# Early q and k without zeros in two halves of rows, early v in one transfer a batch

## The chip, the cores and the metric

The kernel runs on one core of a Trainium2 chip. The metric is the device time of one execution in microseconds; the median of the runs is compared. The engines are TensorE (PE, with its weight loads as PEld), VectorE (DVE), ScalarE (ACT), GpSimd (POOL) and SyncE (SP), which issues nearly all transfers.

## The reference

Causal attention with a bias from cumulated sums, then two gated expert layers, the first behind an RMS norm:

```python
# q, k, v: (4, 8, 576, 64), s: (4, 8, 576)
scores = q @ k.T / 8
bias = -(cum[:, :, :, None] - cum[:, :, None, :])      # cum = cumsum(max(s, 0))
scores = where(causal, -1e9, scores + minimum(bias, 0))
x = softmax(scores) @ v                                # to (2304, 512)
xn = x / sqrt(mean(x * x) + 1e-6) * rms_g
y = (silu(xn @ w_gate) * (xn @ w_val)) @ w_out         # d_ff = 1536
out = (silu(y @ w2_gate) * (y @ w2_val)) @ w2_out
```

## The kernel before, in words

The 2304 tokens are cut so that the first 128 queries of each batch are done first, as "early" attention. They need only the first 128 keys, so a group of four heads fits into one PSUM bank. Such a group is a quad (class `EarlyQuad`); there are eight, two for each of the four batches. With their result the first expert layer starts (`moe1("E", ...)`), while the remaining queries (class `Head`, `Unit`, `PairTile`) are attended batch by batch beside it. The later stages (the second half of the first layer and the second layer, by a scheme of seven products) are not touched.

A quad does the following. `load` brings its q and k. `scores` (line 918) makes, for each head, a matmul of q with k (line 922) and one of the bias (line 925, from the tile `heights`, which holds cumulated sums of s), then on VectorE a reduction that adds the mask and takes the row's least (line 930), and on ScalarE the exponential (line 935). `values` transposes the four results on TensorE (line 947), copies them (lines 951 and 952), multiplies them by v (line 956), and copies the result into x (lines 966 and 967). Two heads share the 128 rows of a tile: an even head has its 64 dimensions on rows 0 to 63, an odd one on rows 64 to 127, and zeros stand in the other half, so that one matmul with the keys of both heads gives only one head's scores. For v it is the same with columns: a head's 64 columns stand beside 64 columns of zeros, and two heads add up in one bank.

Before the change, q and k of a quad (`qe`) come from the host with the zeros: 128 rows of six blocks of 128 columns, 384 KB in one transfer (line 910). v comes in two transfers a batch (line 914, 128 KB each, in pieces of 256 B, even and odd heads), into a tile in which a set-up operation, `pad` (line 530), has put the zeros: two memsets of 128x256.

After four quads, and again after the last four, `normalise` makes the RMS norm for two batches: squares on ScalarE (line 990), sums on TensorE (line 997), small steps on VectorE (lines 1050 to 1081) with a power on GpSimd (line 1084), a transposition (line 1093), a spreading matmul (line 1104), then the scaled x and its two parts xH and xL (lines 1108, 1111, 1113). The expert layer's matmuls are line 1124. For the first five of its twelve slices of 128 hidden columns (HALVES = 5), these 512 tokens are taken in two halves of 256, so that the first half can start before the second normalisation is done.

Weights come as 64-bit numbers, two transfers of 512 KB a slice (line 473), and are converted by ScalarE (477, 484), VectorE (479, 488) or GpSimd (485, 488). Their raw tiles use places that are free early: slice 4's raw places are those of the v of batches 0 and 1, slice 5's those of the v of batches 2 and 3, and slices 6 to 9 have those of the quads' q and k.

The order on every engine is written by a planner (class `Plan`), which runs when the kernel is built. Each call of `op` names an engine (or several, the first free one takes it; a second choice stands 1e6 behind in due time), a cost in ns, what is read and written, and a due time `pri`. The planner plays the program through with these costs and always gives a free engine the ready operation with the least due time. The engines then run their lists strictly in that order. SP is one of them: its transfers are issued in the planner's order, and a transfer that must wait holds those behind it. Due times that matter here: quad i has 2i, its value part 2i - 0.6, its loads 2i - 1000; the load of v of a batch had the load's time of its first quad plus 1; weight slice 0 has -990, slices 1 to 4 -985.9, -985.8, -985.7 and -985.6, later ones -982.6 and up; the expert layer 1e4. Set-up operations come by their due time too: `ident` -1.4e6, the bias's `units_` -1.35e6, `mask` -1.3e6, the pads -1.2e6, `cumulate` (the cumulated sums, VectorE, as soon as s is there) -1e6, two clears of conversion places (cvy, line 495) 2, two clears of xH (line 543) 4.5. The planner takes s as there at once, since the ACT queue's transfer costs it 450 ns. Sixteen fillers (line 1256, identity matmuls with due time 1e9, two instructions each) go where the planner sees TensorE idle after the fourth quad. Eleven warm-up matmuls (line 557) precede the first quad.

Of the kernel before, what the change touches and what calls it, by code (L numbers as in the profile page):

```python
# [23 lines left out]
P = 128  # L24
# [309 lines left out]
def tile_kernel(  # L334
# [174 lines left out]


    early_q = [buf("w", f"{z}{f}", [P, 6, P], F32, "eq") for f in range(8, KF) for z in "HL"]
    early_v = [buf("w", f"{z}{f}", [P, NH, 2, D], F32, "ev") for f in (6, 7) for z in "HL"]
    early = [buf("at", f"pTB{i}", [P, 1536], F32, f"early{i}") for i in range(2)]
    early_p = [Part(b, "p", lambda t: t[:, 1024:1536]) for b in early]
    cum = Part(early[0], "cum", lambda t: t[:NB * NH, :S])
# [6 lines left out]
    def setup():  # L522
# [1 line left out]
            make_identity(nc, ident())  # L524
        op(POOL, 700, make_const, w=[ident], pri=-1.4e6)
        op(POOL, 100, lambda en: en.memset(minus_half(), -0.5), w=[minus_half], pri=-0.8e6)
        for i, v in enumerate(early_v):
            def pad(en, v=v):
                for z in range(2):
                    en.memset(v()[:, z::2, 1 - z], 0.0)  # L530
            op([(POOL, 520), (DVE, 620)], 0, pad, w=[(v, "pad")], pri=-1.2e6 + i)

        def units_(en):
            en.memset(f32(unit()[64:]), 0.0)
# [359 lines left out]
    class EarlyQuad:  # L894
# [12 lines left out]

        def load(self, pri):
            b, ql, vl = self.b, self.ql, self.vl
            op(SP, 4 * P * 768, lambda en: en.dma_start(out=ql(), in_=qe[b, self.j]),  # L910
               w=[ql], pri=pri)
            if self.j == 0:
                for z in range(2):
                    op(SP, 6 * P * 256, lambda en, z=z: en.dma_start(
                        out=vl()[:, z::2, z], in_=ve[b, :, z]), w=[(vl, z)], pri=pri + 1 + 0.1 * z)

        def scores(self, pri):
            pt = ps_ring("sps", 2)
            for h in range(4):
                c = slice(P * h, P * h + P)  # L920
                n = 4 * self.i + h
                op(PE, 0.422 * 4 * P, lambda en, h=h, c=c: en.matmul(
                    pt()[:, c], self.ql()[:, h], self.ql()[:, 4 + h // 2],
                    start=True, stop=False), r=[self.ql], w=[pt], pri=pri)
                op(PE, C_TR, lambda en, c=c, n=n: en.matmul(
                    pt()[:, c], unit()[:, n:n + 1].to_broadcast([P, P]), cumHL(),
                    start=False, stop=True), r=[unit, cumHL, (heights, "clear")], w=[pt], pri=pri)
            for h in range(4):
                c = slice(P * h, P * h + P)
                op(DVE, c_tt(P), lambda en, h=h, c=c: en.tensor_tensor_reduce(  # L930
                    out=self.sc()[:, c], in0=pt()[:, c], in1=mask(), scale=-SCALE, scalar=3.0e38,
                    op0=ALU.add, op1=ALU.min, accum_out=self.col()[:, 0, h:h + 1]),
                   r=[pt, mask], w=[(self.sc, h), (self.col, h)], pri=pri)
                g = 4 * self.j + h
                op(ACT, c_act(P, 2) + 35, lambda en, h=h, c=c, g=g: en.activation(
                    self.sc()[:, c], self.sc()[:, c], ACTF.Exp, scale=-1.0,
                    bias=self.col()[:, 0, h:h + 1],
                    accum_out=self.tot()[:, self.b % 2, g:g + 1]),
                   r=[(self.sc, h), (self.col, h)],
                   w=[(self.sc, h), (self.tot, (self.b, g)), *([f"early {self.i}"] if h == 3 else [])],  # L940
                   pri=pri)

        def values(self, pri):
            pt = ps_ring("tp", 2)
            for h in range(4):
                c = slice(P * h, P * h + P)
                op(PE, C_TR, lambda en, c=c: en.transpose(pt()[:, c], self.sc()[:, c], ident()),
                   r=[(self.sc, h), ident], w=[pt], pri=pri)
            p = self.p
            op([(ACT, c_act(512)), (DVE, c_tt(512))], 0, {  # L950
                ACT: lambda en: en.activation(p(), pt(), ACTF.Copy),
                DVE: lambda en: en.tensor_copy(p(), pt())}, r=[pt], w=[p], pri=pri)
            po = mo_bank()
            for h in range(4):
                c = slice(P * (h // 2), P * (h // 2) + P)
                op(PE, 0.422 * 4 * P, lambda en, h=h, c=c: en.matmul(
                    po()[:, c], self.vl()[:, 4 * self.j + h].rearrange("p z d -> p (z d)"),
                    p()[:, P * h:P * h + P], start=h % 2 == 0, stop=h % 2 == 1),
                   r=[self.vl, p], w=[po], pri=pri)

            x, k, q = self.x.bufs[0], 2 * self.j, P * self.b

            def out():
                return x()[:, k:k + 2, q:q + P], po()[:, :2 * P].rearrange("p (k c) -> p k c", k=2)
            op([(ACT, c_act(256)), (DVE, c_tt(256))], 0, {
                ACT: lambda en: en.activation(*out(), ACTF.Copy),
                DVE: lambda en: en.tensor_copy(*out())},
               r=[po], w=[key for g in range(2) for key in self.x.keys(k + g, (self.b,))], pri=pri)
# [986 lines left out]
```

## Time and profile before

| | |
|---|---|
| time, median of 3 runs | 1030.57 us (1030.27 to 1032.48) |
| time of the profiled execution | 1033.18 us |
| its span | 1030.9 us |
| TensorE busy | 1021.2 us, 99% of the span |
| VectorE, ScalarE, GpSimd busy | 764.9, 631.9, 265.3 us |
| granted TensorE clock | full speed in all 40 slices |
| DMA over the span | 212.07 MB, 206 GB/s |

The profile comes from one execution; what lies between its span and its time is start and end. A busy TensorE is not always useful: fillers and warm-up count as busy. The engine lists are in order, so an instruction that waits holds all behind it on its engine. In the timeline rows below, the columns are the start in us, the duration in us, engine, line, operation, output and inputs, the shape, the number of instructions merged into the row, and in brackets the idle time ahead of it and what ended it. SPq rows are issues of transfers.

### The profile page before, as it was taken

The numbers are of one execution on the slowest core, as the hardware profiler recorded it, in microseconds if no ns is written. First come the engines' busy times: TensorE is split into PE (matmuls) and PEld (weight loads), VectorE is DVE, ScalarE is ACT, GpSimd is POOL, SyncE is SP. The second block draws the span as 40 slices with busy tenths as digits, with TensorE's granted clock in tenths as the row PEclk, the third lists the DMA queues.
The fourth block names the chain that finished last, engine by engine and source line by source line (L and its number), as shares of the span: only waits on it lengthen the run. The fifth ranks groups of instructions, "written<-read, shape, count | busy, mean of one in ns | idle before, by whom it ended". The sixth has DMA issues, their size and how long they took to land.

```text
span 1030.9 us, 17596 instructions
## 1 busy us (share of the span) xinstructions
PE 1021.2 (99%) x5546; PEld 901.6 (87%) x5546; DVE 764.9 (74%) x1748; ACT 631.9 (61%) x1315; POOL 265.3 (26%) x357
## 2 busy tenths in 40 slices
PE   9999999999999999999999999999999999999998
PEld 9998889999999999899888889888888888778888
DVE  7899887677778796568889896566768667866462
ACT  6889876766677465334567765455655445665653
POOL 3678754444344430100000000212211022200000
PEclk9999999999999999999999999999999999999999
DMA  9874534343444773488888643756757766888772
GB/s 330 276 255 136 186 120 121 121 137 105 122 132 146 219 251 139 148 250 297 267 295 274 215 147 101 248 203 211 255 185 248 267 219 232 296 274 254 214 241 94
DMA packets 122717, 212.07 MB, mean 206 GB/s; under 512 B 19008, under 2 KB 46912, under 8 KB 122624
## 3 DMA queue, kind: packets, MB, share of 16 engines
q1 hardware_dynamic: 122288, 210.61, 62.6%
q8 instruction: 44, 0.72, 0.3%
q14 instruction: 49, 0.40, 0.1%
q10 hardware_dynamic: 336, 0.34, 0.1%
HBM read 146.33 MB, written 64.56 MB: 205 GB/s over the span
## 4 chain that ended last, share of the span: by engine, by line
PE 86%; DMA 6%; DVE 5%; issue 1%; ACT 1%; SPq 1%; POOL 0%; DVEq 0%; ACTq 0%; POOLq 0%
PE mo L1124 24%; PE mo L1486 9%; PE mo L1667 9%; PE sps L1667 7%; PE sps L1486 6%; PE tp L1486 6%; PE tp L794 4%; PE sps L712 3%; PE tp L782 3%; PE mo L1743 2%; DMA raw<-in_w_gv 2%; PE mo L1540 2%; PE sps L1124 1%; PE tp L1124 1%; PE sps L837 1%
## 5 line engine op out<-in xcount | busy, mean ns | idle before, releaser
L1124 PE MATMUL mo<-xH,L 128*128 128x448 f32 (+2 forms) x472 | 170.2, 361 | 0.2 <-DVE L L488 0.2
L1124 PE MATMUL mo<-xL,H 128*128 128x448 f32 (+2 forms) x472 | 169.5, 359 | 0.5 <-DVE xL L1113 0.5
L1124 PE MATMUL mo<-xH,H 128*128 128x448 f32 (+2 forms) x472 | 169.4, 360 | 0.0
L749 ACT ACTIVATE sc<-sc,col 128x256 f32<-128x256 f32 (+2 forms) x96 | 60.6, 632 | 59.2 <-DVE col L738 58.7
L1124 PEld LDWEIGHTS mo<-xL,H 128*128 128x128 f32 x472 | 88.9, 188 | 6.0 <-DVE xL L1113 0.7
L1124 PEld LDWEIGHTS mo<-xH,L 128*128 128x128 f32 x472 | 88.9, 188 | 5.9 <-DVE L L488 0.4
L1124 PEld LDWEIGHTS mo<-xH,H 128*128 128x128 f32 x472 | 88.8, 188 | 5.0
L1406 DVE TENSOR_TENSOR hL<-hh,hH 128x512 fp32r<-128x512 f32 (+1 forms) x96 | 64.2, 673 | 38.0 <-ACT hH L1403 37.3
L1403 ACT ACTIVATE hH<-hh 128x512 fp32r<-128x512 f32 (+1 forms) x96 | 57.6, 603 | 52.2 <-DVE hL L1406 20.4
L1486 PE MATMUL mo<-hH,wo 128*128 128x512 f32 x208 | 68.6, 390 | 0.0
L787 DVE TENSOR_TENSOR pTB<-tp,pTB 128x512 fp32r<-128x512 f32 (+1 forms) x96 | 56.3, 597 | 14.3 <-ACT pTB L785 13.6
L1673 ACT ACTIVATE u<-sps 128x512 f32<-128x512 f32 x48 | 28.5, 594 | 53.3 <-PE sps L1667 51.3
L785 ACT ACTIVATE pTB<-tp 128x512 fp32r<-128x512 f32 (+1 forms) x96 | 48.5, 517 | 14.5 <-PE tp L782 13.8
L794 PEld LDWEIGHTS tp<-pTB,vst 128*128 128x128 f32 x320 | 52.9, 189 | 4.2 <-DVE pTB L787 0.8
L794 PE MATMUL tp<-pTB,vst 128*128 128x448 f32 (+3 forms) x320 | 55.3, 314 | 0.1
L782 PE MATMUL tp<-ident,sc 128*128 128x128 f32 x320 | 51.3, 273 | 0.1
L1682 ACT ACTIVATE u<-u 128x512 f32<-128x512 f32 x48 | 29.5, 631 | 32.4 <-DVE u L1677 32.4
L1630 POOL TENSOR_TENSOR tmp<-x,x 128x512 f32<-128x512 f32 x2 | 2.6, 1298 | 171.9 <-DVE x L1502 115.5
L1486 PEld LDWEIGHTS mo<-hH,wo 128*128 128x128 f32 x208 | 39.1, 188 | 8.1
L726 POOL TENSOR_SCALAR_AFFINE_SELECT sc<-cb 128x128 f32<-128x128 f32 x96 | 35.6, 386 | 38.7 <-PE tp L782 37.7
L782 PEld LDWEIGHTS tp<-ident,sc 128*128 128x128 f32 x320 | 39.6, 140 | 6.3 <-PE mo L1124 0.4
L738 DVE CUSTOM_DVE_ANT_0 sc<-sps,cb 128x256 f32<-128x256 f32 (+2 forms) x96 | 35.6, 383 | 11.7 <-PE sps L712 11.6
(318 smaller groups left out, 3017.8 us busy)
## 6 DMA issues: line engine op xcount, KB each, us to landing
raw<-in_w_gv SPq DMA_DIRECT2D x44, 511.8 KB, 5.9
tb<-h_d SPq DMA_DIRECT2D x48, 256.0 KB, 3.4
t<-tb SPq DMA_DIRECT2D x48, 256.0 KB, 3.0
lq<-in_qk SPq DMA_DIRECT2D x32, 288.0 KB, 3.9
cb<-cum_d SPq DMA_DIRECT2D x32, 288.0 KB, 3.7
h<-t SPq DMA_DIRECT2D x32, 256.0 KB, 3.3
h<-h_d SPq DMA_DIRECT2D x24, 256.0 KB, 3.6
row0B<-u SPq DMA_DIRECT2D x24, 256.0 KB, 3.5
```

Source lines behind the costliest of these rows:

```text
L726: op(POOL, 165 + 0.85 * m, lambda en: en.affine_select(out=sc()[:m, o:o + m], in_=cb()[:m, o:o + m], pattern=[[-1, m]], base=0, compare_op ...
L738: op(DVE, c_tt(w), lambda en: en.tensor_tensor_reduce(out=sc()[:m, c:c + w], in0=pt()[:m, c - at:c - at + w], in1=bias()[:m, c + off:c + o ...
L749: op(ACT, c_act(o + m, 2) + 35, lambda en: en.activation(sc()[:m, :o + m], sc()[:m, :o + m], ACTF.Exp, scale=-1.0, bias=col()[:m, 0, t:t + 1],
L782: op(PE, C_TR, lambda en, pt=pt, a=a, kb=kb, t=t: en.transpose(pt()[:, a * P:a * P + P], self.sc[t]()[:, kb * P:kb * P + P], ident()), r=[ ...
L785: op(ACT, c_act(n), lambda en, pt=pt, c=c: en.activation(place(H, c), source(pt, c), ACTF.Copy), r=[pt], w=[(H, c)], pri=pri)
L787: op(DVE, c_tt(n), lambda en, pt=pt, c=c: en.tensor_tensor(out=place(L, c), in0=source(pt, c), in1=f32(place(H, c)), op=ALU.subtract), r=[ ...
L794: op(PE, c_mm(n), lambda en, w=w, z=z, kb=kb, d0=d0, n=n, o=o: en.matmul(po()[:, o:o + n], vst[j]()[:, kb, :], pT[z]()[:, d0:d0 + n], star ...
L1124: op(PE, c_mm(n), lambda en, a=a, x=x, c=c, k=k, i=i: en.matmul(ps()[:, :n], a()[:, c], x(k, lo, n), start=(k == 0 and i == 0), stop=(k == ...
L1403: op(ACT, c_act(n) + 35, lambda en: en.activation(H(), src(), ACTF.Copy), r=[src, *after], w=[H], pri=pri)
L1406: lambda en: en.tensor_tensor(out=L(), in0=src(), in1=f32(H()), op=ALU.subtract),
L1486: op(PE, c_mm(n), lambda en, m=m, w=w, xx=xx, kk=kk, i=i: en.matmul(ps[m]()[:, :n], w(), xx(), start=first and kk == 0 and i == 0, stop=kk ...
L1667: op(PE, c_mm(n), lambda en, w=w, xx=xx, cut=cut, kk=kk, i=i: en.matmul(ps()[:, :n], W[w]()[:, cut], xx(), start=first and kk == 0 and i == 0,
```

## The change

Three things change. The zeros of q and k no longer come from the host: a quad's tile of six blocks is loaded in two transfers of 64 rows and four blocks each (128 KB), and eight `pad` operations (two memsets of 64x256 each) set the zeros on the chip. The matmuls take the same shapes from other blocks. v of a batch comes in one transfer of 384 KB, 3 KB a row, with a block of zeros between the two heads of a pair; no pad is needed for it. Its due time is the first quad's load plus 2.5 instead of plus 1, and the pads have -1.3e6 and -1.3e6 + 1 for the first two quads and 2i - 3.5 for the others.

```diff
--- before.py
+++ after.py
@@ -509,7 +509,7 @@
 
 
     early_q = [buf("w", f"{z}{f}", [P, 6, P], F32, "eq") for f in range(8, KF) for z in "HL"]
-    early_v = [buf("w", f"{z}{f}", [P, NH, 2, D], F32, "ev") for f in (6, 7) for z in "HL"]
+    early_v = [buf("w", f"{z}{f}", [P, NH // 2 * 3 * D], F32, "ev") for f in (6, 7) for z in "HL"]
     early = [buf("at", f"pTB{i}", [P, 1536], F32, f"early{i}") for i in range(2)]
     early_p = [Part(b, "p", lambda t: t[:, 1024:1536]) for b in early]
     cum = Part(early[0], "cum", lambda t: t[:NB * NH, :S])
@@ -524,11 +524,12 @@
             make_identity(nc, ident())
         op(POOL, 700, make_const, w=[ident], pri=-1.4e6)
         op(POOL, 100, lambda en: en.memset(minus_half(), -0.5), w=[minus_half], pri=-0.8e6)
-        for i, v in enumerate(early_v):
-            def pad(en, v=v):
-                for z in range(2):
-                    en.memset(v()[:, z::2, 1 - z], 0.0)
-            op([(POOL, 520), (DVE, 620)], 0, pad, w=[(v, "pad")], pri=-1.2e6 + i)
+        for i, q in enumerate(early_q):
+            def pad(en, q=q):
+                en.memset(q()[D:, :2], 0.0)
+                en.memset(q()[:D, 4:], 0.0)
+            op([(POOL, 540), (DVE, 400)], 0, pad, w=[(q, "pad")],
+               pri=-1.3e6 + i if i < 2 else 2 * i - 3.5)
 
         def units_(en):
             en.memset(f32(unit()[64:]), 0.0)
@@ -907,12 +908,18 @@
 
         def load(self, pri):
             b, ql, vl = self.b, self.ql, self.vl
-            op(SP, 4 * P * 768, lambda en: en.dma_start(out=ql(), in_=qe[b, self.j]),
-               w=[ql], pri=pri)
+            for z in range(2):
+                op(SP, 4 * D * 512, lambda en, z=z: en.dma_start(
+                    out=ql()[D * z:D * z + D, 2 * z:2 * z + 4], in_=qe[b, self.j, D * z:D * z + D]),
+                   w=[(ql, z)], pri=pri + 0.1 * z)
             if self.j == 0:
-                for z in range(2):
-                    op(SP, 6 * P * 256, lambda en, z=z: en.dma_start(
-                        out=vl()[:, z::2, z], in_=ve[b, :, z]), w=[(vl, z)], pri=pri + 1 + 0.1 * z)
+                op(SP, 4 * P * 768, lambda en: en.dma_start(out=vl(), in_=ve[b]), w=[vl],
+                   pri=pri + 2.5)
+
+        def values_of(self, h):
+
+            at = 3 * D * (2 * self.j + h // 2) + D * (h % 2)
+            return self.vl()[:, at:at + 2 * D]
 
         def scores(self, pri):
             pt = ps_ring("sps", 2)
@@ -920,7 +927,7 @@
                 c = slice(P * h, P * h + P)
                 n = 4 * self.i + h
                 op(PE, 0.422 * 4 * P, lambda en, h=h, c=c: en.matmul(
-                    pt()[:, c], self.ql()[:, h], self.ql()[:, 4 + h // 2],
+                    pt()[:, c], self.ql()[:, 4 * (h % 2) + h // 2], self.ql()[:, 2 + h // 2],
                     start=True, stop=False), r=[self.ql], w=[pt], pri=pri)
                 op(PE, C_TR, lambda en, c=c, n=n: en.matmul(
                     pt()[:, c], unit()[:, n:n + 1].to_broadcast([P, P]), cumHL(),
@@ -954,7 +961,7 @@
             for h in range(4):
                 c = slice(P * (h // 2), P * (h // 2) + P)
                 op(PE, 0.422 * 4 * P, lambda en, h=h, c=c: en.matmul(
-                    po()[:, c], self.vl()[:, 4 * self.j + h].rearrange("p z d -> p (z d)"),
+                    po()[:, c], self.values_of(h),
                     p()[:, P * h:P * h + P], start=h % 2 == 0, stop=h % 2 == 1),
                    r=[self.vl, p], w=[po], pri=pri)
 
@@ -1920,17 +1927,19 @@
         cut = 448 - 64 * z
         qk[:, z::2, :, 0, :cut - P] = q[:, z::2, :, P:cut]
         qk[:, z::2, :, 0, cut + 64 - P:QW] = q[:, z::2, :, cut:]
-    qe = np.zeros((NB, 2, 2, D, 6, P), q.dtype)
+    qe = np.zeros((NB, 2, 2, D, 4, P), q.dtype)
     for z in range(2):
-        qe[:, :, z, :, z:4:2] = q[:, z::2, :, :P].reshape(NB, 2, 2, D, P).transpose(0, 1, 3, 2, 4)
-        qe[:, :, z, :, 4:] = (qk[:, z::2, :, 1, :P].reshape(NB, 2, 2, D, P)
-                              .transpose(0, 1, 3, 2, 4))
-    qe = qe.reshape(NB, 2, P, 6, P)
+        qe[:, :, z, :, 2 * z:2 * z + 2] = (q[:, z::2, :, :P].reshape(NB, 2, 2, D, P)
+                                           .transpose(0, 1, 3, 2, 4))
+        qe[:, :, z, :, 2 - 2 * z:4 - 2 * z] = (qk[:, z::2, :, 1, :P].reshape(NB, 2, 2, D, P)
+                                               .transpose(0, 1, 3, 2, 4))
+    qe = qe.reshape(NB, 2, P, 4, P)
+    vz = np.zeros((NB, P, NH // 2, 3, D), v.dtype)
+    vz[:, :, :, ::2] = v[:, :, :P].reshape(NB, NH // 2, 2, P, D).transpose(0, 3, 1, 2, 4)
     arrays = {
         "qk": np.ascontiguousarray(np.concatenate([qk, qk], axis=2)),
         "qe": qe,
-        "ve": np.ascontiguousarray(
-            v[:, :, :P].reshape(NB, NH // 2, 2, P, D).transpose(0, 3, 2, 1, 4)),
+        "ve": vz.reshape(NB, P, NH // 2 * 3 * D),
         "vp": np.ascontiguousarray(vp.reshape(NB, NH, 5, P, D).transpose(0, 1, 3, 2, 4)),
         "s": np.ascontiguousarray(inputs["s"].reshape(NB * NH, S)),
         "w_gv": raw(gv(inputs["moe_w_gate"], inputs["moe_w_val"])),
```

## Rows read from the trace of the kernel before

**Rows 1.** The page, part 1: an engine's busy us, share of span, instructions.

```profile
PE 1021.2 (99%) x5546; PEld 901.6 (87%) x5546; DVE 764.9 (74%) x1748; ACT 631.9 (61%) x1315; POOL 265.3 (26%) x357
```

**Rows 2.** The windows: stretch, busy us (instructions) PE, PEld, DVE, ACT, POOL, clock, DMA.

```profile
5.20:10.00 4.80, 3.90 (x35) 3.60 (x33) 3.36 (x19) 1.86 (x9) 2.29 (x10) 1.00 0.99 331
10.00:15.00 5.00, 5.00 (x48) 5.00 (x48) 4.08 (x21) 3.20 (x17) 0.00 (x0) 1.00 1.08 378
...
35.00:40.00 5.00, 5.00 (x44) 4.98 (x44) 4.68 (x14) 4.99 (x11) 0.98 (x2) 1.00 0.95 293
```

**Rows 3.** TensorE's waits, whole span: waited us in total, times, longest.

```profile
PE sps L922 <- DMA eq<-in_qe: 0.7, 1, 0.7
...
PE mo L1124 <- DVE xL L1113: 0.5, 1, 0.5
```

**Rows 4.** Groups of instructions, 0 to 36 us: the fillers; busy us, mean ns.

```profile
L1256 PE MATMUL mo<-ident 128*128 128x128 f32 x30 | 4.6, 280 | 0.0
```

**Rows 5.** TensorE's timeline, 5 to 12 us.

```profile
5.90 0.30 PE L925 MATMUL sps<-heights 128*128 128x128 f32 x1 [0.25 <-DVE heights L579]
...
6.90 0.31 PE L925 MATMUL sps<-heights 128*128 128x128 f32 x1
7.86 0.49 PE L922 MATMUL sps<-eq 128*128 128x128 f32 x2 [0.65 <-DMA eq<-in_qe]
...
9.25 0.41 PE L947 MATMUL tp<-ident,sc 128*128 128x128 f32 x2
```

**Rows 6.** The timeline of 0 to 25 us: VectorE's rows.

```profile
3.78 0.66 DVE L572 TENSOR_SCALAR early<-early 32x128 f32<-32x128 f32 x1 [2.12 <-DMA early<-in_s]
...
5.48 0.28 DVE L579 TENSOR_TENSOR heights<-cum,heights 32x128 fp32r<-32x128 f32 x1
...
5.87 0.55 DVE L530 MEMSET ev<- 128x256 f32 x2
...
6.47 0.48 DVE L495 MEMSET cvy<- 128x512 f32 x1
...
7.01 0.48 DVE L543 MEMSET xH<- 128x512 f32 x1
7.42 0.24 DVE L930 CUSTOM_DVE_ANT_0 sc<-sps,mask 128x128 f32<-128x128 f32 x1
```

**Rows 7.** The same: ScalarE's first exponential.

```profile
7.70 0.40 ACT L935 ACTIVATE sc<-sc,col 128x128 f32<-128x128 f32 x1 [5.25 <-DVE col L930]
```

**Rows 8.** GpSimd's rows of the timeline, 0 to 70 us.

```profile
2.39 1.06 POOL L530 MEMSET ev<- 128x256 f32 x4
...
20.70 0.88 POOL L485 TENSOR_SCALAR H<-raw 128x512 fp32r<-128x512 f32 x1 [12.24 <-DVE raw L479]
```

**Rows 9.** TensorE's timeline, 30 to 62 us: last values, expert matmuls.

```profile
30.40 0.39 PE L956 MATMUL mo<-early,ev 128*128 128x128 f32 x2
...
33.84 1.14 PE L956 MATMUL mo<-early,ev 128*128 128x128 f32 x8
34.73 0.36 PE L1124 MATMUL mo<-xH,H 128*128 128x256 f32 x1
...
49.67 0.28 PE L1124 MATMUL mo<-xH,H 128*128 128x256 f32 x1
```

**Rows 10.** DMA of 9 to 12 and of 12 to 15 us.

```profile
DMA packets 1514, 1.10 MB, mean 367 GB/s; under 512 B 1245, under 2 KB 1245, under 8 KB 1514
...
DMA packets 363, 1.19 MB, mean 397 GB/s; under 512 B 55, under 2 KB 55, under 8 KB 363
```

**Rows 11.** SP's timeline: issues of v (ev), and of weights (raw).

```profile
11.58 1.06 SPq L914 DMA_DIRECT2D ev<-in_ve  x2
...
20.56 0.33 SPq L473 DMA_DIRECT2D raw<-in_w_gv  x1
```

**Rows 12.** Line L650, 100 to 400 us (64 rows, 128 KB): issue to landing.

```profile
DMA to landing us min/median/max: 2.5/3.1/4.9
```

**Rows 13.** Tile vl (128 rows, 160 KB), 0 to 400 us: issue to landing.

```profile
DMA to landing us min/median/max: 2.1/3.4/7.2
```

## The prediction

> **What bounds the kernel now.** I read the page first: TensorE is busy 99% of the span [rows 1], so the end moves only by what changes in TensorE's unfilled time, or in work that it does without need. The edit touches the first 35 us. The table by stages shows TensorE short of work for 0.9 us between 5.2 and 10 us and full from 10 to 15 us [rows 2]. Its list of waits names two that matter here: 0.7 us for a load of early q and k, and 0.5 us on the second early normalisation [rows 3]. Everything the change could save outright lies in these and in the fillers (line 1256: identity matmuls issued where the planner saw nothing ready), 30 instructions up to 36 us [rows 4]; value matmuls of the same shape take 0.89 us for 8 from start to start [rows 9], so 30 hold TensorE some 3.3 us.
>
> The timeline of TensorE gives the first 10 us: the first quad's bias matmul starts at 5.90 us, the moment `heights` is there; the quad's last one starts at 6.90; TensorE then stands 0.65 us until the second quad's q and k land at 7.86; the first transposition starts at 9.25 [rows 5]. On VectorE the cumulated sums wait until 3.78 us for s to land, `heights` is finished at 5.76, three clears follow (ev, cvy, xH), and the first score reduction starts at 7.42 [rows 6]. ScalarE's first exponential starts 0.28 us behind it [rows 7].
>
> **Part 1, q and k.** A quad's load shrinks from 384 to 256 KB and becomes two issues; the second quad's data is moved ahead of the first batch's v. Ahead of its landing stand 0.58 MB (with s) instead of 1.12 MB, and its second issue is the fourth on SP, at about 2.2 us, where the whole load was issued before. The wait of 0.65 us [rows 5] goes: **-0.65 us**. The first quad gains nothing, since it waits for `heights`, whose s is a transfer of its own. SP issues 20 loads of early q, k and v instead of 16, 0.5 us each [rows 11]; it runs ahead of the transfers, which queue behind one another, so I cost the four at nothing; uncovered they would be 2 us.
>
> **Part 2, zeros.** Four pads become eight, each still two memsets of 256 columns. The planner gives them to the first free of GpSimd and VectorE in order of due time. I walked its list by hand for the order alone: with its own costs it puts v pads on both engines just as the trace has them [rows 6, 8], so the walk can be trusted for the new list. It gives: VectorE pad 0 before the sums; then, behind `heights`, pads 2, 3 and 6, one cvy clear and both xH clears, six operations instead of three. GpSimd gets pads 1, 4, 5 and 7 and a cvy clear, before 5.5 us; it has nothing of weight until 20.70 [rows 8], so those cost nothing, and only its fences would be late if that cover were gone. The planner piles six on VectorE because it believes s there at once and quad 0's scores late; on the chip s lands at 3.78 and the pile comes behind it. A pad takes 0.60 us from start to start, a clear 0.54 or 0.41 to 0.48 [rows 6]: 5.87 + 3 x 0.60 + 0.54 + 0.48 + 0.43 = 9.1 us for the first reduction instead of 7.42, **1.7 us later**. What is queued behind it: exponentials, transpositions, and the third quad's scores, which need the first quad's bank back. TensorE ends the second quad's scores at 7.21 + 1.39 = 8.6 and then wants the first transposition. In the trace that one starts 1.55 us behind the first exponential [rows 5, 7], because it stands behind the second quad's scores; it needs only some 0.7 us (the exponential's 0.40 and a hand-over like the 0.28). So 9.1 + 0.28 + 0.7 = 10.1 against 9.25. Parts 1 and 2 together: **+0.85 us**; ends -0.65 (no pile, if the pads go elsewhere) and +1.7 (the whole delay).
>
> **Part 3, later quads.** From 10 us on TensorE is full [rows 2], so earlier data buys no time by itself, but it changes the order: the fourth quad's load stands 2.0 us earlier in the planner's list, so its scores can come ahead of a block of value matmuls (8 instructions, 0.9 us) [rows 9] and the first normalisation, which sets where the expert layer starts (34.73), may come up to 0.9 us sooner. Ends 0 and -0.9; I take **-0.4**, the middle, as nothing shows it.
>
> **Part 4, v.** It grows from 1.05 to 1.57 MB, but in rows of 3 KB instead of 256 B. The DMA moved 1.10 MB in 3 us with small packets among it and 1.19 without [rows 10]: 0.23 us lost on some 0.32 MB, 0.75 us over all of v. With 0.52 MB less in sum, 1.3 us at 397 GB/s, the stream of loads is some 2.1 us ahead. TensorE's list of waits names no weight load [rows 3], so this is hidden: 0; ends 0 and -0.5 (the wait of L1124 in full, if the normalisation stands behind conversions).
>
> The place matters more. The last batch's v gets due time -985.5; weight slices 1 to 4 have -985.9 to -985.6. So it moves from behind the seventh quad's load (issued 11.58) to behind six to eight weight transfers of 512 KB, one of which waits for a tile that the fourth quad's value matmuls release (issued 20.56) [rows 11]. It is issued at 21 to 22 us and lands some 6 us later, at 27 to 28. The seventh quad's values ran at 30.40 [rows 9], so in the old order nobody waits. But the planner now expects that load later than the start of the expert layer, and will put the last two quads' values, 1.8 us, behind some of its first matmuls; the second normalisation follows them, 4 to 5 us later than now. TensorE has half-width expert work of 5 slices x 24 matmuls, at 44 instructions in 5.00 us [rows 2] 13.7 us, from 34.73 to about 48.5, and second-half work starts at 49.67 [rows 9]: the cover ends about where the second half begins. Beyond it stand attention's first scores. Ends: -0.5 (the 0.5 us wait on that normalisation [rows 3]) and +4 (no cover). I take **0**, nearer to the lower end: moved work is no added work, VectorE can convert weights in the meantime, and TensorE's biggest gap near there now is the 0.5 us of [rows 3].
>
> The sum: 0.85 - 0.4 + 0 + 0 = **+0.45 us** on the profiled execution (span 1030.9, 1033.18 us in all). That execution lies 2.6 us above the median of the runs shown; on the median, 1030.57, it gives **1031.0 us**. A measurement tells 0.2%, 2.1 us, from no change: forecast "no difference".
>
> [...] In the trace, single loads onto 64 rows of 128 KB land in a median of 3.1 us [rows 12], those onto 128 rows of 160 KB in 3.4 [rows 13]: no sign that half the rows cost more. [...]
>
> **The rivals.** (a) *Slower: the last v comes too late.* The mechanism of part 4: the second normalisation falls behind the end of the half-width work at 49 us. It decides once that normalisation is over 3 us later than now and attention's first scores aren't ready. Price: +2.5 to +4 instead of 0, so 1033.5 to 1035 us, 1034 in the middle. For it: cover and need meet at 49. Against: VectorE then converts weights earlier instead. Chance 0.26. (b) *Slower: half-row loads go at half speed.* If they did, 2.1 MB of q and k, 5.3 us at the 397 GB/s of [rows 10], would take 10.6, and the last v would land near 33, some 2.4 us behind 30.40: 1031.0 + 2.4 = 1033.4. [...] Chance 0.04. (c) *Faster: the early order tightens.* No pile counts (the pads hide in the wait for s), the 0.65 us and the waits in [rows 3] go, and fillers fall into waits where they now hold up work: -0.65 - 0.5 - 0.9 - 0.7 (a fifth of the fillers) = -2.75, so 1027.8. For it: 3.3 us of fillers stand ahead of the normalisation's small steps. Against: their number is fixed. Chance 0.22. (d) *The change doesn't do what it says*: it surely moves the bytes, but the zeros could be set without standing in anyone's way, all on GpSimd. Then parts 1 and 2 give -0.65 and the sum is -1.05, 1029.5, inside the forecast. VectorE's share in [rows 6] speaks against it.
>
> **How the numbers follow.** Forecast within 0.2%: 0.48, its own range 1029.0 to 1032.6 (2 us to either side of it, less where a and c begin). Slower 0.30 (a and b), faster 0.22 (c). The range takes in most of a and c: 1027.6 to 1034.6.
>
> **What would show it.** Right: no wait of L922 on a load; six VectorE memsets behind `heights` and a first reduction near 9.1; TensorE idle some 1.5 us between 8.5 and 10.2; the last ev load issued past 20 us; value matmuls of early quads behind the first L1124; the second normalisation some 4 us later in the order. Wrong: the first reduction at 7.5 still (part 2), values of all quads before L1124 (part 4), or TensorE idle over 4 us between 40 and 60.

## The result, and the profile after

The changed kernel takes **1042.62 us** (median of 4 runs, 1041.29 to 1043.43) against 1031.28 us for the kernel before on the same chip (4 runs): ratio **1.0102**, interval 1.0089 to 1.0114. It is slower by 1%; the prediction said no difference, at most 1034.6. The profiled execution has a span of 1041.4 us and 1043.43 us in all.

The page, part 1, of the changed kernel [rows 1]:

```profile
PE 1026.4 (99%) x5546; PEld 903.2 (87%) x5546; DVE 775.9 (74%) x1759; ACT 628.4 (60%) x1311; POOL 259.3 (25%) x358
```

TensorE executes the same 5546 matmuls, in a span that is 10.5 us longer: 5.2 us more busy, the rest idle. Its waits, all of the span (waited us, times, longest) [rows 3]:

```profile
PE sps L713 <- DVE col L739: 2.3, 3, 1.3
PE tp L795 <- DVE pTB L788: 1.2, 2, 0.9
...
PE tp L954 <- ACT sc L942: 0.8, 1, 0.8
...
PE sps L929 <- POOL H L485: 0.5, 1, 0.5
```

The wait on a load of q and k is gone, as intended (L929 was L922). In its place stand several others: attention's scores and values wait for VectorE (2.3 and 1.2 us in sum), the first early transposition (L954) and a late quad's scores stand 0.8 and 0.5 us. None is near 10 us. The windows show where TensorE falls behind (its busy us and instructions, clock, DMA share, GB/s) [rows 2]:

```profile
0.00:30.00 30.00, 27.54 (x221) 1.00 0.91 295
30.00:60.00 30.00, 28.65 (x215) 0.94 0.86 284
60.00:100.00 40.00, 37.18 (x250) 1.00 0.52 162
100.00:200.00 100.00, 99.33 (x568) 1.00 0.43 138
```

The same windows of the kernel before:

```profile
0.00:30.00 30.00, 28.06 (x234) 1.00 0.98 338
30.00:60.00 30.00, 28.48 (x227) 1.00 0.85 281
60.00:100.00 40.00, 39.81 (x259) 1.00 0.52 163
100.00:200.00 100.00, 100.00 (x585) 1.00 0.46 140
```

By 100 us before has issued 234 + 227 + 259 = 720 matmuls, after 686; between 100 and 200 us another 17 are missing. At the 5.85 matmuls a microsecond of the last row these 51 are some 8.7 us (an estimate, since their sizes differ): most of the loss, and it has no single place. The clock's 0.94 in 30 to 60 us is of the profiled execution alone: the other three show a clock of 1.0 and 1041.29 to 1043.35 us.

TensorE's timeline after [rows 5, 9]; L932 was L925, L963 was L956, L1131 was L1124, L1004 is the sums of the normalisation:

```profile
5.50 0.30 PE L932 MATMUL sps<-heights 128*128 128x128 f32 x1
...
8.94 0.33 PE L954 MATMUL tp<-ident,sc 128*128 128x128 f32 x1 [0.79 <-ACT sc L942]
...
35.23 0.38 PE L963 MATMUL mo<-early,ev 128*128 128x128 f32 x2
...
35.67 0.36 PE L1131 MATMUL mo<-xH,H 128*128 128x256 f32 x1
...
42.07 1.05 PE L1004 MATMUL mo<-half,sq 128*128 128x2 f32 x8 [0.28 <-DVE t L1140]
44.17 1.05 PE L1004 MATMUL mo<-half,sq 128*128 128x2 f32 x8 [0.23 <-ACT sq L997]
```

VectorE's timeline after [rows 6]:

```profile
2.73 0.22 DVE L573 TENSOR_SCALAR early<-early 32x128 f32<-32x128 f32 x1 [0.87 <-DMA early<-in_s]
...
4.17 0.28 DVE L580 TENSOR_TENSOR heights<-cum,heights 32x128 fp32r<-32x128 f32 x1
4.56 0.27 DVE L529 MEMSET eq<- 64x256 f32 x1
...
7.93 0.27 DVE L530 MEMSET eq<- 64x256 f32 x1
8.13 0.22 DVE L937 CUSTOM_DVE_ANT_0 sc<-sps,mask 128x128 f32<-128x128 f32 x1
```

SP's issues after [rows 11]; the last load of v stands behind eight transfers of weights:

```profile
14.92 7.40 SPq L473 DMA_DIRECT2D raw<-in_w_gv  x8
22.46 0.34 SPq L916 DMA_DIRECT2D ev<-in_ve  x1
```

The first 10 us are as forecast in kind, and better in size. The sums of the second normalisation come at 42.07 and 44.17; in the kernel before they ran at 32.94 and 36.90:

```profile
32.94 1.04 PE L997 MATMUL mo<-half,sq 128*128 128x2 f32 x8
...
36.90 0.95 PE L997 MATMUL mo<-half,sq 128*128 128x2 f32 x8
```

Three theories followed. **A:** the late last v pushes the second normalisation, and with it the loss. **B:** the pads on VectorE hold up the start. **C:** the planner writes another list from the new operations, and other lists are worse than that of before in many small places, whatever the change does on the chip.

### The profile page after: what moved, and what is told of

The parts are those of the page before. It is cut to its first block, busy times and chain, and to the rows that moved or that the text cites. A ratio compares the mean times of both kernels' runs of the same rounds, so it can differ in the third digit from the quotient of the medians.

```text
span 1041.4 us, 17622 instructions
## 1 busy us (share of the span) xinstructions
PE 1026.4 (99%) x5546; PEld 903.2 (87%) x5546; DVE 775.9 (74%) x1759; ACT 628.4 (60%) x1311; POOL 259.3 (25%) x358
## 4 chain that ended last, share of the span: by engine, by line
PE 65%; DVE 13%; DMA 13%; issue 4%; ACT 3%; SPq 2%; POOL 1%; DVEq 0%; ACTq 0%; POOLq 0%
PE mo L1131 17%; PE mo L1493 9%; PE mo L1674 7%; PE tp L1493 5%; PE sps L1674 5%; PE sps L1493 5%; PE tp L795 4%; DMA cvs<-in_w_o 3%; PE tp L783 3%; PE sps L713 2%; DMA raw<-in_w_o 2%; DMA raw<-in_w_gv 2%; PE mo L1750 2%; PE mo L1547 2%; DMA tb<-h_d 2%
## 5 line engine op out<-in xcount | busy, mean ns | idle before, releaser
L1131 PE MATMUL mo<-xH,H 128*128 128x448 f32 (+2 forms) x472 | 170.2, 362 | 0.3 <-DVE t L1140 0.3
L1131 PE MATMUL mo<-xL,H 128*128 128x448 f32 (+2 forms) x472 | 169.7, 360 | 0.4 <-DVE xL L1120 0.4
L1131 PE MATMUL mo<-xH,L 128*128 128x448 f32 (+2 forms) x472 | 169.9, 361 | 0.0
L1131 PEld LDWEIGHTS mo<-xH,H 128*128 128x128 f32 x472 | 89.3, 190 | 6.3 <-DVE t L1140 0.5
L1131 PEld LDWEIGHTS mo<-xL,H 128*128 128x128 f32 x472 | 89.5, 190 | 5.9 <-DVE xL L1120 0.6
L1131 PEld LDWEIGHTS mo<-xH,L 128*128 128x128 f32 x472 | 89.5, 190 | 5.4
L1138 ACT ACTIVATE t<-mo 128x448 f32<-128x448 f32 (+2 forms) x59 | 30.4, 515 | 29.8 <-PE mo L1131 27.3
L1140 DVE SCALAR_TENSOR_TENSOR t<-t,mo 128x448 f32<-128x448 f32 (+2 forms) x59 | 34.8, 590 | 17.8 <-ACT t L1138 15.0
```

The lines of the kernel that those rows point to most:

```text
L1131: op(PE, c_mm(n), lambda en, a=a, x=x, c=c, k=k, i=i: en.matmul(ps()[:, :n], a()[:, c], x(k, lo, n), start=(k == 0 and i == 0), stop=(k == ...
L1138: op(ACT, c_act(n), lambda en: en.activation(t()[:, :n], gp()[:, :n], ACTF.Tanh, scale=0.5), r=[gp], w=[t], pri=pri)
L1140: op(DVE, c_tt(n), lambda en: en.scalar_tensor_tensor(out=t()[:, :n], in0=t()[:, :n], scalar=1.0, in1=gp()[:, :n], op0=ALU.add, op1=ALU.mu ...
```

## First experiments: undo one thing in the changed kernel

**v ahead of the raw slices** (theory A undone):

```diff
-                   pri=pri + 2.5)
+                   pri=pri + 2.05)
```

> The changed kernel with early v due at the first quad's load plus 2.05 instead of plus 2.5: the last batch's v is issued ahead of the transfers of weight slices 1 to 4 again, the pads stay as changed. Theory A (late v: the last v stands behind eight weight transfers, so the planner puts the second early normalisation behind weight conversions, and the half-width expert work runs out before it): back to 1031 to 1034 us. Theory B (pads on VectorE hold up the first score reductions): stays at 1040 to 1043. Theory C (any other order of the early part costs or gains some us by chance, and the loss has no single place): anything from 1030 to 1043, with the loss not tied to the second normalisation.

Measured: 1037.68 us, ratio 1.0051 (1.0031 to 1.0071). The second normalisation's sums are back at 32.75 and 36.98 us, and half of the loss is gone; theory A's range, 1031 to 1034, is missed.

**Pads on GpSimd alone** (theory B undone):

```diff
-            op([(POOL, 540), (DVE, 400)], 0, pad, w=[(q, "pad")],
+            op(POOL, 540, pad, w=[(q, "pad")],
```

> The changed kernel with all eight pads on GpSimd alone; the order of SP's transfers stays that of the changed kernel, v is as late. Theory A: 1041 to 1043, at most 0.7 us faster than the changed kernel (the first reduction starts at about 7 instead of 8.13 us). Theory B: 1031 to 1035. Theory C: anything between.

Measured: 1040.0 us, 1.0073 (1.0054 to 1.0092), between the ranges of A and B. The pile is gone (first reduction at 7.19 us instead of 8.13, first transposition at 8.20 instead of 8.94), most of the loss is not.

**Both edits:**

> The changed kernel with both: v due at plus 2.05 and the pads on GpSimd alone. Theory A and B: 1029 to 1033, by A no more than 1 us faster than with v alone moved. Theory C: not below the kernel before other than by chance.

Measured: 1038.49 us, 1.0067 (1.0044 to 1.009). With both suspects gone most of the loss stays, and the second edit gives nothing on top of the first. Neither A nor B is enough.

**The kernel before with v late** (A alone, in the old kernel):

```diff
-                        out=vl()[:, z::2, z], in_=ve[b, :, z]), w=[(vl, z)], pri=pri + 1 + 0.1 * z)
+                        out=vl()[:, z::2, z], in_=ve[b, :, z]), w=[(vl, z)], pri=pri + 2.5 + 0.1 * z)
```

> The kernel before with nothing changed but the due time of v's two loads, the first quad's load plus 2.5 and 2.6 instead of plus 1 and 1.1, so that the last v stands behind the weight transfers; q and k with their zeros, pads of v as before. Theory A: 1036 to 1042. Theory B: 1030 to 1032. Theory C: anything between, with the loss spread.

Measured: 1039.46 us, 1.0066 (1.0043 to 1.0089); the sums come at 43.95 and 46.02. Taken alone it looks like a proof of A. But each of these four edits also makes the planner write a new list, so the next question was what a new list costs by itself.

## The parts alone, and lists without any change

**v's part alone**: the kernel before, with one transfer of 384 KB a batch, zeros from the host, no pads of v, due time as before (of its edit the load alone is shown).

```diff
-                for z in range(2):
-                    op(SP, 6 * P * 256, lambda en, z=z: en.dma_start(
-                        out=vl()[:, z::2, z], in_=ve[b, :, z]), w=[(vl, z)], pri=pri + 1 + 0.1 * z)
+                op(SP, 4 * P * 768, lambda en: en.dma_start(out=vl(), in_=ve[b]), w=[vl],
+                   pri=pri + 1)
```

> The kernel before with the values' part of the change alone: v of a batch comes in one transfer of 384 KB with zeros from the host, due where it was due before (after the first quad), no pads of v on the chip; q and k as before. Theory A (the last v behind the raw slices is the loss): v is not late here, so 1030 to 1033. Theory B (pads of q and k on VectorE): they are untouched, 1030 to 1032. Theory C (any other list of the early work costs some us, and the loss has no place of its own): 1034 to 1041, although nothing is late.

Measured: **1031.05 us** against 1032.3, ratio **0.999** (0.9981 to 0.9999; 10 runs). The planner happens to write the same lists here: TensorE's and ScalarE's are those of before entry by entry, so the run says nothing on C. It is the only kernel tried whose median lies under that of before, by 0.1%, at the edge of the noise.

**q's and k's part alone**: two halves of rows, pads on the chip; v as before (of its edit the load alone is shown).

```diff
-            op(SP, 4 * P * 768, lambda en: en.dma_start(out=ql(), in_=qe[b, self.j]),
-               w=[ql], pri=pri)
+            for z in range(2):
+                op(SP, 4 * D * 512, lambda en, z=z: en.dma_start(
+                    out=ql()[D * z:D * z + D, 2 * z:2 * z + 4], in_=qe[b, self.j, D * z:D * z + D]),
+                   w=[(ql, z)], pri=pri + 0.1 * z)
```

> The kernel before with the part on q and k alone: two halves of rows without zeros, pads set on the chip; v as before. Theory A: v is not late, 1030 to 1033. Theory B: the whole pile of pads is here, 1035 to 1042. Theory C: 1034 to 1041.

Measured: 1041.05 us, 1.0079 (1.0062 to 1.0095). A's range is missed. It is another list, but B is at work here too: with the pads of v still there, twelve memsets of pads and two clears stand on VectorE behind `heights`, the first reduction starts at 10.69 us, and TensorE waits for the first transposition:

```profile
11.50 0.45 PE L955 MATMUL tp<-ident,sc 128*128 128x128 f32 x1 [3.15 <-ACT sc L943]
```

That is some 3 of the 8.8 us lost; in the changed kernel the same wait is 0.79.

**Two lists without any change of work**: one constant of the planner's model is touched, so that the engines get the same operations on the same data in another order, and a few of them on another engine (with the other landing time VectorE has 1750 instructions instead of 1748, ScalarE 1311 instead of 1315, GpSimd 359 instead of 357).

```diff
-            done = 2300.0 + took - ns + slow
+            done = 2250.0 + took - ns + slow
```

> The kernel before with one constant of the planner's changed, the landing time that it assumes for a transfer, 2300 to 2250: the same instructions on the same data, only listed in another order. Theories A and B: nothing that they name is touched, 1030 to 1032. Theory C: the order of before is a good draw and another one costs some us, 1033 to 1042.

```diff
-C_TR = 110
+C_TR = 112
```

> The kernel before with the planner's price of a transpose 110 changed to 112: the same instructions on the same data, only listed in another order. Theories A and B: 1030 to 1032. Theory C: 1033 to 1042, and another time than the run with the other constant.

Measured: **1041.97 us, 1.0093** (1.0077 to 1.0108) and **1043.45 us, 1.0101** (1.0086 to 1.0116). The second of them lies above C's range too. Nothing that A or B names is touched or late, and the whole loss is there: the first reduction starts at 7.50 and 7.43 us (7.42 in before), and the sums of the second normalisation at 32.21 and 36.78 with the other transpose price and, with the other landing time, at

```profile
33.46 0.95 PE L997 MATMUL mo<-half,sq 128*128 128x2 f32 x8
...
35.41 0.95 PE L997 MATMUL mo<-half,sq 128*128 128x2 f32 x8
```

This is what told the theories apart.

The places differ. TensorE's longest waits with the other landing time:

```profile
PE sps L712 <- DVE col L738: 3.4, 3, 2.0
PE mo L1104 <- DVE x L1108: 3.0, 1, 3.0
```

and with the other transpose price:

```profile
PE tp L794 <- DVE pTB L787: 3.3, 1, 3.3
```

The windows of the run with the other landing time show the clock around its wait of 3.0 us:

```profile
40.00:50.00 10.00, 6.78 (x46) 0.84 1.02 388
50.00:60.00 10.00, 10.00 (x72) 0.82 0.61 203
```

TensorE stands still for 3.2 us of 40 to 50, at a granted clock of 0.84 in the mean of that window, and in the next 10 us works, fully busy, at 0.82. In the kernel before, no window up to 200 us shows a clock under 1.0.

**More draws**: the changed kernel with either constant, and before with a third value.

> The changed kernel with the planner's price of a transpose 110 changed to 112, another list of the same work. Theory C: some other time, 1033 to 1046, not that of the changed kernel (1042.6) but for chance. Theory A (the last v is still late): 1041 to 1044.

Measured: 1038.19 us, 1.0056 (1.0037 to 1.0074).

> The changed kernel with the planner's assumed landing time 2300 changed to 2250, another list of the same work. Theory C: some other time, 1033 to 1046. Theory A: 1041 to 1044.

Measured: 1049.55 us, 1.0173 (1.0144 to 1.0203), above both ranges.

```diff
-C_TR = 110
+C_TR = 108
```

> The kernel before with the planner's price of a transpose 110 changed to 108, a third list of the same work. Theory C: 1033 to 1044, as with the other two constants. If the loss with those two were a misfortune of theirs and the list of before an ordinary one: 1029 to 1033.

Measured: 1036.09 us, 1.0042 (1.0029 to 1.0055).

Lists other than that of before, with v late or not: the work of before takes 1.0042, 1.0066, 1.0093 and 1.0101, in the mean 1.0076; the work of the change 1.0051, 1.0056, 1.0067, 1.0073, 1.0102 and 1.0173, in the mean 1.0087. The two groups lie over each other, and none of the ten reaches the list of before. (The part on q and k alone, with its wait of 3.15 us, is left out.) Nor does a late second normalisation go with the loss: its sums begin at 32 to 34 us in the two lists at 1.0093 and 1.0101, and at 40.79 in the one at 1.0042.

## All of the change in the list of before

To see what the work itself costs, the planner is given the operations and prices of before. One planned load issues both halves; each of the four planned pads of v clears the pads of two quads instead; v is due as before, so the late place of the last v goes with the changed kernel's list. (The edit of the load alone is shown.)

```diff
+            def halves(en):
+                for z in range(2):
+                    en.dma_start(out=ql()[D * z:D * z + D, 2 * z:2 * z + 4],
+                                 in_=qe[b, self.j, D * z:D * z + D])
+            op(SP, 4 * P * 768, halves, w=[(ql, "rows")], pri=pri)
```

> All of the change on the chip (q and k in two halves of rows without zeros, pads set by memset, v of a batch in one transfer with zeros), but the planner is given the operations and prices of the kernel before: one planned operation issues both halves, each of the four planned pads of v clears two quads' pads instead, v is due where it was due before. TensorE's and ScalarE's lists are then those of before, entry by entry. Theory C (the list is the loss, not the work): 1029 to 1032. A rival, that the transfers or pads themselves cost what was lost: 1035 to 1043. Theory B (pads on VectorE): four of the memset pairs are still on VectorE ahead of the first reduction, 1033 to 1037.

Measured: **1034.48 us**, ratio **1.0023** (1.0012 to 1.0034; 10 runs). Read from the traces, TensorE's and ScalarE's lists are those of before entry by entry. The time lies above C's range and in B's: of the 1.0% the list takes some 0.8, the late v with it; 2.4 us stay with the work. Its windows say where they can come from:

```profile
4.00:8.00 4.00, 4.00 (x30) 1.00 0.86 279
8.00:12.00 4.00, 3.93 (x34) 1.00 1.04 262
12.00:16.00 4.00, 4.00 (x38) 1.00 1.05 294
16.00:20.00 4.00, 4.00 (x38) 1.00 1.06 259
...
45.00:60.00 15.00, 12.17 (x78) 0.77 0.87 299
```

The same windows of v's part alone, where q and k come in whole rows:

```profile
4.00:8.00 4.00, 3.80 (x32) 1.00 1.04 408
8.00:12.00 4.00, 4.00 (x37) 1.00 1.03 394
...
45.00:60.00 15.00, 13.71 (x99) 1.00 0.78 269
```

TensorE counts as busy from 4 to 8 us (4.00 instead of 3.80), but with 30 matmuls instead of 32, and its first transposition starts at 8.48 us instead of 8.25: nothing is gained at the start. While half rows are in the queue, the DMA engines are as busy from 8 us on and move 262 GB/s between 8 and 12 us instead of 394. The bytes saved are lost again, and what follows is later: the block of six weight loads goes out at 36.00 us instead of 33.59. SP's row with v's part alone,

```profile
33.59 3.45 SPq L473 DMA_DIRECT2D raw<-in_w_gv  x6
```

and with all of the change in the same list:

```profile
36.00 3.17 SPq L473 DMA_DIRECT2D raw<-in_w_gv  x6
```

Behind it stands a store of ScalarE's tile t. ScalarE's row with v's part alone,

```profile
46.93 0.38 ACT L1130 ACTIVATE t<-mo 128x256 f32<-128x256 f32 x1 [1.96 <-DMA h_d<-t]
```

and with all of the change in the same list:

```profile
50.16 0.38 ACT L1141 ACTIVATE t<-mo 128x256 f32<-128x256 f32 x1 [4.74 <-DMA h_d<-t]
```

TensorE has nothing else in its list there:

```profile
51.05 0.80 PE L1266 MATMUL mo<-ident 128*128 128x128 f32 x2 [2.15 <-DVE t L1143]
```

Between 50 and 55 us, a stretch that begins with the last microsecond of this wait, the clock is 0.52; all ten executions of this kernel show 0.997 or 0.998 over the span, those of v's part alone 1.0.

Three runs bear on the rate. **Whole rows in the list of before**: each quad's q and k in one transfer of 128 rows by 2 KB (the pads, as many and as large, then lie on the last two blocks of all rows).

```diff
-                for z in range(2):
-                    en.dma_start(out=ql()[D * z:D * z + D, 2 * z:2 * z + 4],
-                                 in_=qe[b, self.j, D * z:D * z + D])
+                en.dma_start(out=ql()[:, 0:4], in_=qe[b, self.j])
```

> As the run with all of the change in the list of before, but each quad's q and k come in one transfer of 128 rows by 2 KB instead of two of 64 rows by 2 KB: the same bytes in packets of the same size, 8 issues fewer; q of the lower rows then lies in other columns than the matmuls assume (this stands in for nothing but the time). Pads are as many and as large. If the half rows slow the queue (there 205 to 290 GB/s between 4 and 22 us, where whole rows had 390 to 418): about 400 GB/s here, raw slices about 2 us earlier, no 2.2 us stall at 49 us, 1029 to 1031. If packets of 2 KB or the pads are what costs: still under 300 GB/s or still 1033 to 1036.

Measured: 1032.69 us, ratio 1.0012 (1.0002 to 1.0021; 10 runs).

```profile
4.00:8.00 4.00, 4.00 (x25) 1.00 1.02 364
8.00:12.00 4.00, 4.00 (x37) 1.00 1.04 382
12.00:16.00 4.00, 4.00 (x38) 1.00 1.03 410
16.00:20.00 4.00, 4.00 (x38) 1.00 1.02 409
```

Same bytes, same 2 KB packets, same pads: the rate is back, and 1.8 us with it by the medians, 1.1 by the ratios, whose intervals overlap. Here the half rows slow the queue (262 GB/s against 382 between 8 and 12 us); 2 KB packets and pads hardly do (382 against 394 with v's part alone). The packets themselves take longer: between 8 and 12 us one of 2 KB took 125 ns in the mean with half rows and 84 with whole ones, and one of v, 3 KB onto whole rows in both, 190 and 125. That there are also twice as many transfers was not tried apart.

Not all of the loss is back: the forecast for half rows alone was 1029 to 1031, and v's part alone stands at 0.9990 in the same list. What the difference of some 2 us is made of is not shown. The pads on VectorE are one candidate, as the first reduction starts at 8.12 us here and at 7.23 with v's part alone.

**Two queues**: the lower halves issued by ScalarE.

```diff
-                for z in range(2):
-                    en.dma_start(out=ql()[D * z:D * z + D, 2 * z:2 * z + 4],
+                for z, q in enumerate((en, nc.scalar)):
+                    q.dma_start(out=ql()[D * z:D * z + D, 2 * z:2 * z + 4],
                                 in_=qe[b, self.j, D * z:D * z + D])
```

> As the run with all of the change in the list of before, but the lower half of each quad's rows is issued by ScalarE's queue, beside the upper half on SyncE's: 8 issues move to ScalarE. If half rows are slow because one half at a time is under way, both halves are under way at once here: over 350 GB/s and 1029 to 1032. If they are slow in themselves, or ScalarE's issues come in the way of its exponentials: 1034 to 1038.

Measured: 1036.16 us, 1.0042 (1.0027 to 1.0057).

```profile
4.00:8.00 4.00, 3.13 (x28) 1.00 1.04 281
8.00:12.00 4.00, 2.04 (x20) 1.00 1.05 229
```

A miss for the idea that two halves under way at once would fill in for each other, as far as this run tries it: both queues moved data up to 8 us, at 281 GB/s against 279 with one queue; then ScalarE's next load was issued at 11.20 us, so the 229 are nearly SyncE's queue alone. TensorE waits (2.2 us once on ScalarE's exponentials, which stand behind a load that ScalarE now issues).

**Whole rows in the changed kernel's own list:**

```diff
-                op(SP, 4 * D * 512, lambda en, z=z: en.dma_start(
-                    out=ql()[D * z:D * z + D, 2 * z:2 * z + 4], in_=qe[b, self.j, D * z:D * z + D]),
+                op(SP, 4 * D * 512, lambda en, z=z: z or en.dma_start(
+                    out=ql()[:, 0:4], in_=qe[b, self.j]),
                    w=[(ql, z)], pri=pri + 0.1 * z)
```

> The changed kernel with its own list, but the first of each quad's two planned transfers brings all 128 rows by 2 KB and the second nothing (q of the lower rows lies in other columns than the matmuls assume). Theory C (its list is most of the loss): 1037 to 1042. If the slow half rows are most of the loss in its own list too: 1030 to 1034.

Measured: 1041.0 us, 1.0091 (1.0068 to 1.0113).

```profile
8.00:12.00 4.00, 2.30 (x20) 0.95 1.04 377
12.00:16.00 4.00, 4.00 (x24) 0.62 1.04 414
```

Rate restored, loss kept, in a list that is that of the changed kernel entry by entry on TensorE. A new wait comes at the start, since s lands later with whole rows, at 3.94 us instead of 2.73. VectorE's first step on it,

```profile
3.94 0.22 DVE L573 TENSOR_SCALAR early<-early 32x128 f32<-32x128 f32 x1 [2.11 <-DMA early<-in_s]
```

and TensorE's first transposition:

```profile
10.05 0.33 PE L954 MATMUL tp<-ident,sc 128*128 128x128 f32 x1 [1.70 <-ACT sc L942]
```

The pile on VectorE ends later by as much (first reduction at 9.24 instead of 8.13), TensorE stands 1.70 us, and the clock is 0.62 after it. So this run does not hold the start fixed: it shows that the rate alone does not bring the time back, not what the half rows cost in this list.

## Why the prediction was wrong

**Part 1** was right: no wait of L929 on a load. (Its 0.58 MB are 0.60, which changes nothing.)

**Part 2** was right on the list and wrong on the start. Six memset operations stand on VectorE behind `heights`, as walked by hand, but s landed 1.05 us earlier (2.73 instead of 3.78), which the sum did not contain, so the first reduction ran at 8.13 instead of 9.1, although the pile took 3.57 us instead of 3.25. The early s goes with the half rows: VectorE's first step on it started at 2.73 to 2.99 us in the eight profiled kernels that load half rows on one queue, at 3.61 to 4.38 in the eight with whole rows, and within one list at 2.86 against 3.61. The first transposition came at 8.94 against 9.25 in before [rows 5]: parts 1 and 2 gave -0.3 us, where the sum had +0.85.

**Part 3** was wrong: the first expert matmul is 0.9 us later (35.67 against 34.73 [rows 9]), not 0.4 sooner.

**Part 4** holds the step that failed: "I take 0 ... moved work is no added work". The bytes of v had the right sign (0 to -0.5; v's part alone in the same list gives 1.25 us less, with an interval from 0.1 to 2). The order was mispriced. The hand walk found the late last v and, behind it, a new place for the second normalisation, and priced that as one move in a list that else stays. The list does not stay: read place by place from the traces, 2132 of TensorE's 5546 matmuls stand at another line or tile than in before, and with the other landing time, without any change of work, 2741. Such a list cost 4 to 10 us in the three runs without any change of work, and some 8 in the changed kernel (1.0102 in its own list, 1.0023 in that of before). The values of all quads still ran before the first L1131, so the detail that I feared did not happen, and the loss came all the same.

**Rival (a)** named the right sign and one true movement (the sums 7 to 9 us later) with too small a price. Whether that movement is the main cause in the changed kernel is not shown: v late in the old kernel costs 7.7 us, v ahead in the new one gives back 4.9, but a constant without meaning costs 4 to 11, in two of three lists with the sums as early as in before.

**Rival (b)** had 0.04 and was true in kind: 262 GB/s against 382 for the same bytes between 8 and 12 us. Its price was 2.4 us, the runs with and without half rows in one list differ by 1.8 (1.1 by the ratios). The way was another: the last v did not hold up its quads there, the later weights and the store behind them did hold up TensorE near 49 us. I argued against it from the wrong rows: [rows 12, 13] are single loads from issue to landing, which say little of the rate when loads stand behind one another. The half speed that it is added up from was a supposition, and no run shows it: between 8 and 12 us the rate fell to 0.69 (262 of 382 GB/s), in a stream in which loads of whole rows stand too. The run with two queues, slow as well, is not explained by these runs.

**Rival (c)** needed fillers and waits to fall away; TensorE waits in more places than before instead.

The forecast would have needed a term for the list itself, of one sign. What stays open is why the list of before is so much better than its neighbours; each of the others loses in places of its own, and no common one was found. One explanation that no run tries: the planner has many constants set by hand, and if they were chosen by the time of this very list, any other would be expected to lose.

## What to carry to other kernels

Where a planner writes the order, an edit of a load or a cost replaces the list of the whole stage: measure what a null edit (a constant of the model by 2%) does before a gain or loss is put down to the edit itself, and to judge the edit, hold the old list and change only what an operation issues. Price transfers to half the rows by the rate of the queue while several stand in it (here 262 GB/s against 382), not by the landing of one [rows 12, 13]. Where the clock falls with a wait on TensorE, count more than the wait: with all of the change in the list of before, the expert matmuls of 256 columns started 0.12 us apart ahead of the wait of 2.15 us and 0.21 us apart behind it, from 52.2 to 56.1 us, at a clock of 0.52 up to 55 us.

## What the runs showed of the hardware

With transfers of 64 rows by 2 KB one behind the other in the queue, among others of whole rows, the stream moved 259 to 294 GB/s between 8 and 20 us at a DMA share of 1.04 to 1.06; with 128 rows by 2 KB in their place, 382 to 410 at 1.02 to 1.04. The two halves on two queues gave 281 between 4 and 8 us, one queue 279. VectorE's first step on s, which waits for its transfer, started 0.75 and 1.21 us later with whole rows in the queue than with half rows in the same list (3.61 against 2.86, 3.94 against 2.73).

With all of the change in the list of before, a wait of 2.15 us on TensorE near 49 us went with a granted clock of 0.52 between 50 and 55 us. It was low without a long wait too: in the profiled execution of the changed kernel the clock was 0.66 between 45 and 50 us, and in the 5 us before TensorE had been busy for 4.50 with no single wait over 0.3.
